# An expert's last tokens computed beside a full slot instead of in a slot of their own

## The chip, the cores and the metric

The kernel runs on one core of a Trainium2 chip. The metric is device time in microseconds. Engines: PE (TensorE, matrix products; PEld is its weight load), ACT (ScalarE), DVE (VectorE), POOL (GpSimd, which here issues indirect DMAs: gathers and scatters by a list of rows), SP (SyncE, which issues the plain DMAs). A name with q (SPq, PEldq) is an engine's queue of instructions: branches, register loads, semaphores.

## What is computed

The reference chains three stages: an attention with a feature map, a dense two-layer network, and a routed one (mixture of experts). The change touches the third alone:

```python
logits = x @ w_gate + modality_bias[modality_id]     # 4608 tokens, 8 experts
e_idx = np.argmax(logits, axis=1)
...
for e in range(E):
    mask = e_idx == e
    h = np.maximum(x[mask] @ w1[e], 0.0)             # 512 -> 1024
    out[mask] = gate_w[mask, None] * (h @ w2[e])     # 1024 -> 512
```

All is float32. With the inputs of the reference the eight experts get 227, 0, 0, 1555, 0, 1831, 994 and 1 tokens.

## The kernel before

Attention and the dense network run first, to about 1300 us. While the last unit of the dense network ends, the tokens are sorted into a table in DRAM, `tab`, one region of rows for each expert, a row being a token's number and its weight. Empty rows carry the number of a token that doesn't exist; its gather reads zeros and its scatter is dropped.

The routed stage works through 25 slots (`NS1`), of up to 256 tokens of one expert each (`T`). A slot is either full, 256 tokens wide, or half, 128 wide. `order` (from L587, on DVE) works out from the eight counts, by some 40 small operations, which expert and which region of `tab` each slot has, and leaves them in `ie` and `io`; `ni` holds how many full and half slots there are. An expert's tokens go into as many full slots as they fill; a rest of at most 128 tokens becomes a half slot, a longer one a full slot. Full slots come first, and 18 slots run whatever the counts (`NS0`). Each later slot stands in a `tc.If` whose condition every engine reads from `ni`: slots 18 to 20 exist in both forms, the full one first (L854) and the half one (L856); slots 21 to 24 in the half form alone. With these inputs there are 18 full slots and three half ones, 18, 19 and 20.

To float32 accuracy each operand is split into a high and a low part (`h`, `l`), and a product is three matmuls. For a slot that means:
- `gather(i)`: SP loads the slot's table rows `mrec`, POOL gathers 256 tokens (two indirect DMAs of 256 KB, `xg`);
- `prep(i)`: eight transposes on PE (`px`), cast and subtraction on ACT and DVE (`xT`);
- `fetch`: 4 MB of weights of the slot's expert by eight plain DMAs from SP into `raw`; `split_steps`: ACT casts each piece to `m` (L658) and DVE subtracts (L659), and after each second one SP issues the fetch of a later slot;
- `body(i)`: 96 matmuls of the first layer (`mh`, L699) and 48 of the second (`po`, L711), 128 of the slot's tokens after the other; ACT scales the output (`o`, L748), POOL scatters it (L749);
- `half(i)`: 24 matmuls of the first layer (`sh`, L724), with ACT's `sr`, eight transposes (`st`), 24 of the second (`sp`, L743).

`hooks(i)` interleaves with slot i's steps the gather for slot i+2, the splits for slot i+1 and, three steps before the end, `prep(i+1)`. The order on each engine is not written out by hand: a scheduler places the instructions of each straight stretch by their data and a model of their times, so that a longer chain on one engine can move others. `tc.If` bounds such a stretch. At an If that is not taken, an engine waits until what it has in flight is done (SP: until its DMAs have landed) and then branches over the block.

Of the kernel before, what the change touches and what calls it, by code (L numbers as in the profile page):

```python
# [940 lines left out]
```

## Time and profile before

| | us |
|---|---|
| median of 3 runs | 1830.23 (1829.14 to 1831.64) |
| profiled execution | 1822.83 |
| its span in the trace | 1820.8 |
| PE busy in the span | 1754.4 (96%) |

The profiled execution is one run with the hardware profiler; all times of rows count from its span's start. Its own time is 7.4 us under the median of the runs. 192.25 MB are moved. Of the 25 slots 21 run: L699 has 1728 matmuls, 96 for each of 18 full slots, and L724 has 72, 24 for each of three half slots. The routed stage's slots 2 to 17 lie between about 1380 and 1756 us, the half slots from 1757 us to the end.

### The profile page before, as it was taken

Reading aid. Unit: us, or ns where it says so; the run is one execution under the profiler, and the core shown is the slowest. Engines: PE = TensorE matmul, PEld = TensorE weight load, DVE = VectorE, ACT = ScalarE, POOL = GpSimd, SP = SyncE. Lnnn points to the kernel's source line nnn. Section 1 sums busy time; section 2 is a strip of 40 time slices with the busy share of each in tenths; the row PEclk is TensorE's granted clock in tenths of the full one; section 3 lists DMA queues with packets and bytes.
Section 4 is the critical chain, followed back from the end, with each engine's and each line's share of the span. In section 5 each row is a group of like instructions: output and inputs, shape, how many; then the busy total and the mean of one; then the engine's idle time right before and its main releaser. Section 6 shows DMA issues by size and latency. Waiting matters only on the chain. (4 is left out here: it accounts for less than half of the span.)

```text
span 1820.8 us, 27482 instructions
## 1 busy us (share of the span) xinstructions
PE 1754.4 (96%) x10038; PEld 1504.2 (83%) x10038; DVE 1110.5 (61%) x1959; ACT 942.9 (52%) x1715; POOL 644.6 (35%) x524
## 2 busy tenths in 40 slices
PE   8999999998789999999999999999898999999996
PEld 7999999997668888888888888888687999999974
DVE  6888877779895454545454545454546655655555
ACT  5777777776643433333433333433426555655555
POOL 0544454447554242425243424242322221211121
PEclk9999999999999999999999999999899999999998
DMA  6334333322420101010101000010309765766666
GB/s 177 108 99 125 109 85 104 102 85 87 132 77 1 47 1 47 1 47 1 46 1 37 11 23 25 18 30 18 122 36 366 274 222 197 248 224 225 230 217 221
DMA packets 143444, 192.25 MB, mean 106 GB/s; under 512 B 64831, under 2 KB 89535, under 8 KB 143298
## 3 DMA queue, kind: packets, MB, share of 16 engines
q1 hardware_dynamic: 135346, 168.82, 28.6%
q0 software_dynamic: 7952, 21.54, 3.6%
q8 instruction: 85, 1.39, 0.3%
q14 instruction: 61, 0.50, 0.1%
HBM read 160.61 MB, written 30.50 MB: 105 GB/s over the span
## 5 line engine op out<-in xcount | busy, mean ns | idle before, releaser
L450 PE MATMUL ph<-x,w 128*128 128x512 f32 x1728 | 429.6, 396 | 11.9 <-DVE fr L468 10.6
L450 PEld LDWEIGHTS ph<-x,w 128*128 128x128 f32 x1728 | 322.8, 189 | 90.0 <-DVE fr L468 13.9
L480 PE MATMUL acc<-gh,w 128*128 128x512 f32 x1152 | 357.2, 392 | 1.6 <-DVE gh L470 1.6
L471 POOL TENSOR_TENSOR gl<-fr,gh 128x512 fp32r<-128x512 f32 x144 | 187.8, 1305 | 360.0 <-DVE gh L470 291.9
L659 DVE TENSOR_TENSOR m<-raw,m 128x512 fp32r<-128x512 f32 x336 | 218.5, 690 | 137.4 <-ACT m L658 133.6
L480 PEld LDWEIGHTS acc<-gh,w 128*128 128x128 f32 x1152 | 218.0, 189 | 47.0 <-DVE gh L470 1.8
L480 PE MATMUL acc<-gl,w 128*128 128x512 f32 x576 | 226.9, 395 | 11.5 <-POOL gl L471 11.5
L658 ACT CAST m<-raw 128x512 fp32r<-128x512 f32 x336 | 195.5, 618 | 74.0 <-PE mh L699 30.3
L463 ACT ACTIVATE n<-ph 128x512 int32<-128x512 f32 x144 | 85.7, 595 | 257.4 <-PE ph L450 254.1
L699 PEld LDWEIGHTS mh<-xT,m 128*128 128x128 f32 x1728 | 210.0, 192 | 3.0 <-DVE m L659 1.2
L699 PE MATMUL mh<-xT,m 128*128 128x256 f32 x1728 | 210.9, 283 | 0.8 <-DVE m L659 0.4
L465 DVE SCALAR_TENSOR_TENSOR fr<-ph,n 128x512 f32<-128x512 f32 x144 | 99.2, 689 | 179.6 <-ACT n L463 177.2
L468 DVE SCALAR_TENSOR_TENSOR fr<-fr,ph 128x512 f32<-128x512 f32 x144 | 98.8, 686 | 164.7 <-ACT fr L467 164.5
L711 PE MATMUL po<-m,hh 128*128 128x512 f32 x576 | 180.9, 395 | 0.0
L466 ACT ACTIVATE fr<-fr 128x512 f32<-128x512 f32 x144 | 91.0, 632 | 147.2 <-DVE fr L465 143.3
L168 PEld LDWEIGHTS kv<-v,ke 128*128 128x128 f32 (+1 forms) x1280 | 146.0, 191 | 13.0 <-issue 7.1
L168 PE MATMUL kv<-v,ke 128*128 128x65 f32 (+1 forms) x1280 | 151.6, 273 | 1.7 <-ACT ke L148 1.6
L749 POOL DMA_INDIRECT out_dram<-o,mrec x39 | 39.6, 1015 | 295.5 <-ACT o L748 247.3
L223 PE MATMUL pn<-qx,kvz 128*128 128x288 f32 x512 | 136.6, 409 | 3.3 <-DVE kvz L179 1.8
L480 PEld LDWEIGHTS acc<-gl,w 128*128 128x128 f32 x576 | 109.5, 190 | 36.0 <-POOL gl L471 13.2
L711 PEld LDWEIGHTS po<-m,hh 128*128 128x128 f32 x576 | 105.9, 189 | 20.1
L223 PEld LDWEIGHTS pn<-qx,kvz 128*128 128x128 f32 x512 | 93.5, 192 | 24.9 <-ACT w L420 2.2
(200 smaller groups left out, 2782.4 us busy)
## 6 DMA issues: line engine op xcount, KB each, us to landing
raw<-in_moe_w_dram SPq DMA_DIRECT2D x179, 512.0 KB
xt<-xo SPq DMA_DIRECT2D x16, 576.0 KB
xr<-xt SPq DMA_DIRECT2D x36, 256.0 KB
raw_k<-in_k_dram SPq DMA_DIRECT2D x32, 256.0 KB
raw_q<-in_q_dram SPq DMA_DIRECT2D x32, 256.0 KB
v<-in_v_dram SPq DMA_DIRECT2D x64, 128.0 KB
st<-in_moe_w_in_dram SPq DMA_DIRECT2D x16, 512.0 KB
st<-in_moe_w_out_dram SPq DMA_DIRECT2D x16, 512.0 KB
```

The costliest lines, as they stand in the source:

```text
L168: nc.tensor.matmul(o,e[p0:p1,idx*256+s*F:idx*256+(s+1)*F],vh[p0:p1,h,cc,:],start=first and h==0 and s==0,stop=last,skip_group_check=True)
L223: nc.tensor.matmul(pn,kz[:,s,h*P:(h+1)*P],qx[:,h,s,su],start=s==0,stop=s==1)
L450: nc.tensor.matmul(ph,A[:,ws],xhl[u,d][k],start=n[0]==0,stop=n[0]==11); n[0]+=1
L465: nc.vector.scalar_tensor_tensor(g,ph,INV2PI,n,op0=ALU.mult,op1=ALU.subtract)
L466: nc.scalar.activation(g,g,AF.Sin,scale=math.pi)
L468: nc.vector.scalar_tensor_tensor(g,g,-0.5,ph,op0=ALU.add,op1=ALU.mult)
L471: nc.gpsimd.tensor_tensor(gl,g,f32(gh),ALU.subtract)
L480: nc.tensor.matmul(accs[u][d],A[:,ws],B,start=(f==0 and k==0),stop=(f==NF-1 and k==2))
L658: nc.scalar.copy(h,a)
L659: nc.vector.tensor_tensor(l,a,f32(h),ALU.subtract)
L699: nc.tensor.matmul(ph[:,f2*T:(f2+1)*T],A[:,ws],B[d//2][:,xs],start=n==0,stop=n==11); n+=1
L711: nc.tensor.matmul(po[c],A[:,ws],B,start=(f==0 and j==0),stop=(f==NF2-1 and j==2))
```

## The change

A rest of at most 128 tokens no longer has a slot of its own where its expert's last full slot is one of the slots 14 (`NX`) to 21: it is computed by a half, `half(i,True)`, that stands in an If right ahead of that slot's `body(i)` (from slot 18 on within the full form's If) and uses the same split weights. `order` sorts the slots into three classes, plain full, full with a rest beside, and half, by tables of 24 entries instead of 16 (some 75 operations, the wide ones cut in two). With these inputs slots 16 and 17 get the rests of 39 and 19 tokens, slot 18 stays a half slot with its one token, and slots 19 and 20 are empty. For slots 14 to 17 `gather` gets a third indirect DMA of 256 KB (`xgx`), and `prep_x` adds four transposes (`pxx`), a cast and a subtraction, whether the half runs or not. The full forms of slots 18 to 21 hold a half too; slot 21 has a full form now.

```diff
-    NS0=NTOK//T; NS1=NS0+NE-1; NSH=(NTOK+NE*(T//2-1))//T-NS0
+    NS0=NTOK//T; NS1=NS0+NE-1; NSH=(NTOK+NE*(T//2-1))//T+1-NS0; NX=14
+    NI=2+NS0-NX+NSH
...
+        at=[0]; room=xtile("fr","order",F32); ge=xtile("fr","order_ge",F32)[0:1,0:13*24].rearrange("p (s k) -> p s k",k=24)
+        def part(w):
+            at[0]+=w
+            return room[0:1,at[0]-w:at[0]]
+        e=part(25); nc.vector.memset(e[:,24:25],0.0)
+        for j in range(3): nc.vector.tensor_copy(e[:,8*j:8*j+8],ei)
         nc.vector.tensor_scalar(ki,ki,0xffff,None,op0=ALU.bitwise_and)
...
+        d=part(8); nc.vector.tensor_tensor(d,tot,nb,ALU.subtract)
+        lo=part(8); nc.vector.memset(lo,1.0); nc.vector.memset(lo[:,0:1],3.0)
+        hx=part(8); nc.vector.tensor_tensor(hx,nb,lo,ALU.is_ge)
+        nc.vector.tensor_tensor(hx,hx,d,ALU.mult)
+        ha=part(8); nc.vector.scalar_tensor_tensor(ha,nb,1.0,d,op0=ALU.is_lt,op1=ALU.mult)
+        nc.vector.tensor_tensor(nb,tot,ha,ALU.subtract); nc.vector.tensor_tensor(nb,nb,hx,ALU.subtract)
...
+        cv=part(1); nc.vector.tensor_reduce(cv,tt,AX.X,ALU.max)
+        kx=part(8); nc.vector.tensor_tensor(kx,px,cv.to_broadcast([1,8]),ALU.is_ge)
+        n=part(24)
+        nc.vector.tensor_tensor(n[:,8:16],kx,hx,ALU.mult)
+        nc.vector.tensor_copy(n[:,16:24],ha)
+        nc.vector.tensor_tensor(nb,nb,hx,ALU.add)
+        nc.vector.scalar_tensor_tensor(n[:,0:8],n[:,8:16],-2.0,nb,op0=ALU.mult,op1=ALU.add)
...
-        for i in (1,2,4,8):
-            t2=small(f"on{i}",0,[1,16]); nc.vector.tensor_copy(t2[:,0:i],end[:,0:i])
-            nc.vector.tensor_tensor(t2[:,i:16],end[:,i:16],end[:,0:16-i],ALU.add)
+        for i in (1,2,4,8,16):
+            t2=part(24); nc.vector.tensor_copy(t2[:,0:i],end[:,0:i])
+            nc.vector.tensor_tensor(t2[:,i:24],end[:,i:24],end[:,0:24-i],ALU.add)
             end=t2
...
         for d_,s_ in ((de,se),(do,so)):
-            nc.vector.tensor_tensor(ge,C["slot"].unsqueeze(2).to_broadcast([1,NS1,16]),end.unsqueeze(1).to_broadcast([1,NS1,16]),ALU.is_ge)
-            nc.vector.tensor_tensor(ge,ge,d_.unsqueeze(1).to_broadcast([1,NS1,16]),ALU.mult)
-            nc.vector.tensor_reduce(s_,ge,AX.X,ALU.add)
+            for s0,s1 in ((0,13),(13,NS1)):
+                g=ge[:,0:s1-s0,:]
+                nc.vector.tensor_tensor(g,C["slot"][:,s0:s1].unsqueeze(2).to_broadcast([1,s1-s0,24]),end.unsqueeze(1).to_broadcast([1,s1-s0,24]),ALU.is_ge)
+                nc.vector.tensor_tensor(g,g,d_.unsqueeze(1).to_broadcast([1,s1-s0,24]),ALU.mult)
+                nc.vector.tensor_reduce(s_[:,s0:s1],g,AX.X,ALU.add)
...
+        ni=small("ni",0,[1,NI],I32)
+        nc.vector.tensor_copy(ni[:,0:1],end[:,15:16]); nc.vector.tensor_copy(ni[:,1:2],end[:,23:24])
+        for n0,n1,i0,k0,k1 in ((2,2+NS0-NX,NX,7,15),(2+NS0-NX,NI,NS0,15,23)):
+            h=part(n1-n0); nc.vector.tensor_scalar(h,C["slot"][:,i0:i0+n1-n0],end[:,k0:k0+1],None,op0=ALU.is_ge)
+            h2=part(n1-n0); nc.vector.tensor_scalar(h2,C["slot"][:,i0:i0+n1-n0],end[:,k1:k1+1],None,op0=ALU.is_lt)
+            nc.vector.tensor_tensor(ni[:,n0:n1],h,h2,ALU.mult)
...
+    def rest(i): return NX<=i<NS0+NSH
+    def alloc_x(i):
+        X["x",i]=tuple(xtile("n",f"xX{k}_{i}") for k in range(2))
     def alloc_g(i):
-        R[i]=sb.tile([P,2,2],I32,tag="mrec",name=f"mrec_{i}",bufs=4)
+        R[i]=sb.tile([P,3,2],I32,tag="mrec",name=f"mrec_{i}",bufs=4)
+        if rest(i): xgs["x",i]=xtile("fr",f"xgx_{i}",F32)
         if i==1:
             xg=S("raw_k","xg_1",F32); xgs[i]=[xg[:,c*512:(c+1)*512] for c in range(2)]
         else: xgs[i]=[xtile("x1T",f"xg_{i}_{c}",F32) for c in range(2)]
-    def gather(i):
+    def gather(i,beside):
         rec=R[i]
-        nc.sync.dma_start(rec,tab[ds(off_[i],T),:].rearrange("(c p) t -> p c t",p=P))
+        nch=3 if beside else 2
+        nc.sync.dma_start(rec[:,0:nch,:],tab[ds(off_[i],nch*P),:].rearrange("(c p) t -> p c t",p=P))
+        if beside: nc.gpsimd.indirect_dma_start(xgs["x",i],None,x1d[:,:],IndirectOffsetOnAxis(ap=rec[:,2,0:1],axis=0))
         for c in range(2):
             nc.gpsimd.indirect_dma_start(xgs[i][c],None,x1d[:,:],IndirectOffsetOnAxis(ap=rec[:,c,0:1],axis=0))
     def prep(i):
...
                     nc.tensor.transpose(pt[:,d*T+c*P:d*T+(c+1)*P],xg[c][:,(2*g+d)*P:(2*g+d+1)*P],ident)
             nc.scalar.copy(h[g],pt)
             nc.vector.tensor_tensor(l[g],pt,f32(h[g]),ALU.subtract)
+    def prep_x(i):
+        h,l=X["x",i]; xg=xgs["x",i]
+        pt=ms(f"pxx_{i}")
+        for d in range(4): nc.tensor.transpose(pt[:,d*P:(d+1)*P],xg[:,d*P:(d+1)*P],ident)
+        nc.scalar.copy(h,pt)
+        nc.vector.tensor_tensor(l,pt,f32(h),ALU.subtract)
...
-    def half(i):
-        xh,xl=X[i]
+    def half(i,beside):
+        if beside:
+            h,l=X["x",i]; x=lambda d: (h[:,d*P:(d+1)*P],l[:,d*P:(d+1)*P])
+        else:
+            h,l=X[i]; x=lambda d: tuple(t[d//2][:,(d%2)*T:(d%2)*T+P] for t in (h,l))
         rs=[]
         for fh in range(2):
             ph=bank("pj",f"sh_{i}_{fh}")
             n=0
             for d in range(4):
-                wh,wl=W[i,0][2*d+fh]; xs=slice((d%2)*T,(d%2)*T+P)
+                wh,wl=W[i,0][2*d+fh]; xh,xl=x(d)
                 for (A,B) in ((xh,wh),(xl,wh),(xh,wl)):
-                    nc.tensor.matmul(ph,A[d//2][:,xs],B,start=n==0,stop=n==11); n+=1
+                    nc.tensor.matmul(ph,A,B,start=n==0,stop=n==11); n+=1
             r=xtile("row",f"sr_{i}_{fh}",F32)
             nc.scalar.activation(r,ph,AF.Relu)
             rs.append(r)
...
             ws=slice((f%4)*P,(f%4+1)*P)
             for j,(A,B) in enumerate(((hh,wh),(hh,wl),(hl,wh))):
                 nc.tensor.matmul(po,A[:,ws],B,start=(f==0 and j==0),stop=(f==NF2-1 and j==2))
-            if f==NF2-1: finish(i,0,po)
+            if f==NF2-1: finish(i,2 if beside else 0,po)
             if f%2==1: yield
...
-    def tokens(i):
+    def tokens(i,beside):
         if i<NS0+2: alloc_g(i)
-        load_off(i); gather(i)
+        load_off(i); gather(i,beside)
...
-            if i+2<NS1: tokens(i+2)
+            if i+2<NS1: tokens(i+2,steps==12 and rest(i+2))
             if i<NS0: alloc(i+1)
+            if NX<=i+1<NS0: alloc_x(i+1)
...
         h[steps-3].append(lambda:prep(i+1))
+        if NX<=i+1<NS0: h[steps-3].append(lambda:prep_x(i+1))
...
     for i in range(1,NS0):
-        if i==NS0-1:
-            loaded=[value(o["n"][0:1,j:j+1],mybir.ALL_ENGINES,NS1,"only compared with constants") for j in range(2+NSH)]
+        if i==NX-1:
+            loaded=[value(o["n"][0:1,j:j+1],mybir.ALL_ENGINES,NS1,"only compared with constants") for j in range(NI)]
+        if i>=NX:
+            with tc.If(loaded[2+i-NX]>0): run(half(i,True),{})
         run(body(i,i),hooks(i,12))
     for i in range(NS0,NS1):
         if i+1<NS1: alloc(i+1)
         if i+2<NS1: alloc_g(i+2)
-        if i<NS0+NSH:
-            with tc.If(loaded[0]>i): run(body(i,i),hooks(i,12))
-        is_half=loaded[2+i-NS0]>0 if i<NS0+NSH else loaded[1]>i
-        with tc.If(is_half): run(half(i),hooks(i,8))
+        if rest(i):
+            with tc.If(loaded[0]>i):
+                alloc_x(i); prep_x(i)
+                run(half(i,True),{})
+                run(body(i,i),hooks(i,12))
+        is_half=loaded[2+NS0-NX+i-NS0]>0 if rest(i) else loaded[1]>i
+        with tc.If(is_half): run(half(i,False),hooks(i,8))
 @with_exitstack
```

On POOL, around the end of slot 1; `xg_2` and `xg_3` are the gathers for slots 2 and 3, `out` from `o_1` the scatters of slot 1's two outputs. Before:

```order
L676 DMA xg_2_0_12559<-x1d_66,mrec_2_12558 128x512
L676 DMA xg_2_1_12560<-x1d_66,mrec_2_12558 128x512
L676 DMA xg_3_0_12607<-x1d_66,mrec_3_12606 128x512
L676 DMA xg_3_1_12608<-x1d_66,mrec_3_12606 128x512
L749 DMA out_0_dram<-o_1_0_12755,mrec_1_11937 4608x512
L749 DMA out_0_dram<-o_1_1_12818,mrec_1_11937 4608x512
L676 DMA xg_4_0_12858<-x1d_66,mrec_4_12857 128x512
L676 DMA xg_4_1_12859<-x1d_66,mrec_4_12857 128x512
```

After:

```order
L716 DMA xg_2_0_12582<-x1d_66,mrec_2_12581 128x512
L716 DMA xg_2_1_12583<-x1d_66,mrec_2_12581 128x512
L798 DMA out_0_dram<-o_1_0_12778,mrec_1_11937 4608x512
L798 DMA out_0_dram<-o_1_1_12841,mrec_1_11937 4608x512
L716 DMA xg_3_0_12630<-x1d_66,mrec_3_12629 128x512
L716 DMA xg_3_1_12631<-x1d_66,mrec_3_12629 128x512
L716 DMA xg_4_0_12881<-x1d_66,mrec_4_12880 128x512
L716 DMA xg_4_1_12882<-x1d_66,mrec_4_12880 128x512
```

The two gathers for slot 3 have moved behind both of slot 1's scatters.

On PE, slot 3's transposes `px_3` (`mh_2` and `po_2` are slot 2's first and second layer). Before, in the middle of slot 2's last 24 matmuls:

```order
L711 MATMUL po_2_1_12982<-m2_3_11969,hh_2_1_12904 128x512 x2
L711 MATMUL po_2_1_12982<-m2_3_11969,hl_2_1_12905 128x512
L684 MATMUL px_3_0_13044<-ident_60,xg_3_0_12607 128x128
L684 MATMUL px_3_0_13044<-ident_60,xg_3_1_12608 128x128
L684 MATMUL px_3_0_13044<-ident_60,xg_3_0_12607 128x128
L684 MATMUL px_3_0_13044<-ident_60,xg_3_1_12608 128x128
L684 MATMUL px_3_1_13051<-ident_60,xg_3_0_12607 128x128
L684 MATMUL px_3_1_13051<-ident_60,xg_3_1_12608 128x128
L684 MATMUL px_3_1_13051<-ident_60,xg_3_0_12607 128x128
L684 MATMUL px_3_1_13051<-ident_60,xg_3_1_12608 128x128
L711 MATMUL po_2_1_12982<-m2_4_11970,hh_2_2_12938 128x512 x2
```

After, from the start of slot 2:

```order
L745 MATMUL mh_2_0_12851<-xT_2_0_12638,m0_0_11950 128x256 x3
L745 MATMUL mh_2_1_12902<-xT_2_0_12638,m0_0_11950 128x256 x3
L745 MATMUL mh_2_0_12851<-xT_2_0_12638,m0_2_11952 128x256 x2
L745 MATMUL mh_2_1_12902<-xT_2_0_12638,m0_2_11952 128x256
L745 MATMUL mh_2_0_12851<-xT_2_0_12638,m0_2_11952 128x256
L745 MATMUL mh_2_1_12902<-xT_2_0_12638,m0_2_11952 128x256 x2
L724 MATMUL px_3_0_13067<-ident_60,xg_3_0_12630 128x128
L745 MATMUL mh_2_0_12851<-xT_2_1_12639,m0_4_11954 128x256 x2
L745 MATMUL mh_2_1_12902<-xT_2_1_12639,m0_4_11954 128x256 x2
L724 MATMUL px_3_0_13067<-ident_60,xg_3_1_12631 128x128
L745 MATMUL mh_2_0_12851<-xT_2_1_12639,m0_4_11954 128x256
L745 MATMUL mh_2_1_12902<-xT_2_1_12639,m0_4_11954 128x256
```

They have moved from the second layer of slot 2 to behind 12 matmuls of its first.

On PE, from slot 13 to slot 14 (`po_13` is slot 13's second layer, `mh_14` slot 14's first). Before:

```order
L711 MATMUL po_13_1_15702<-m1_6_11964,hl_13_3_15693 128x512
L711 MATMUL po_13_1_15702<-m1_7_11965,hh_13_3_15692 128x512 x2
L711 MATMUL po_13_1_15702<-m1_7_11965,hl_13_3_15693 128x512
L699 MATMUL mh_14_0_15795<-xT_14_0_15586,m0_0_11950 128x256 x3
L699 MATMUL mh_14_0_15795<-xT_14_0_15586,m0_2_11952 128x256 x3
```

After, with the transposes of the 128 tokens beside and the If:

```order
L730 MATMUL pxx_14_15877<-ident_60,xgx_14_15354 128x128 x4
L757 MATMUL po_13_1_15801<-m1_5_11963,hl_13_2_15758 128x512
L757 MATMUL po_13_1_15801<-m1_6_11964,hh_13_3_15791 128x512 x2
L757 MATMUL po_13_1_15801<-m1_6_11964,hl_13_3_15792 128x512
L757 MATMUL po_13_1_15801<-m1_7_11965,hh_13_3_15791 128x512 x2
L757 MATMUL po_13_1_15801<-m1_7_11965,hl_13_3_15792 128x512
L575 TENSOR_LOAD ni_0_12572
L901 COMPARE_AND_BRANCH
L773 MATMUL sh_14_0_15902<-m0_0_11950,xX0_14_15685 128x512
L773 MATMUL sh_14_0_15902<-m0_0_11950,xX1_14_15686 128x512
L773 MATMUL sh_14_0_15902<-m0_0_11950,xX0_14_15685 128x512
```

Between the two slots there are now a register load, a branch and the half's matmuls `sh_14`; the eight transposes `px_14` stand a few rows ahead of `pxx_14`, as they did before.

## Rows read from the trace of the kernel before

**Rows 1.** Table by stretch: its length, busy PE, PEld, DVE, ACT, POOL; clock, DMA.

```profile
1639.60:1662.70 23.10, 23.10 (x152) 21.18 (x152) 13.78 (x23) 13.52 (x24) 4.20 (x5) 1.00 0.66 229
1757.40:1772.60 15.20, 13.53 (x64) 10.52 (x64) 12.23 (x20) 12.12 (x23) 4.54 (x3) 1.00 0.72 230
1772.60:1795.20 22.60, 15.79 (x64) 12.33 (x64) 12.31 (x20) 12.20 (x23) 3.93 (x3) 0.85 0.78 274
```

**Rows 2.** Waits, 1400 to 1757 us: who for whom, total us, times, longest.

```profile
PE mh L699 <- issue: 0.4, 1, 0.4
```

**Rows 3.** PE in order of time, slots 18 to 20: start, us, operation [idle before].

```profile
1757.44 5.71 PE L724 MATMUL sh<-m,xT 128*128 128x512 f32 x24 [1.28 <-ACTq L854]
1762.99 0.60 PE L732 MATMUL st<-ident,sr 128*128 128x128 f32 x4
1764.41 0.66 PE L732 MATMUL st<-ident,sr 128*128 128x128 f32 x4 [0.82 <-ACT sr L726]
...
1768.02 1.03 PE L684 MATMUL px<-ident,xg 128*128 128x128 f32 x8
1768.81 0.71 PE L743 MATMUL sp<-m,sg 128*128 128x512 f32 x2
...
1771.40 0.39 PE L743 MATMUL sp<-m,sl 128*128 128x512 f32 x1
1772.66 0.73 PE L724 MATMUL sh<-m,xT 128*128 128x512 f32 x2 [0.87 <-ACTq L854]
...
1813.60 0.39 PE L743 MATMUL sp<-m,sl 128*128 128x512 f32 x1
```

**Rows 4.** ACT in order of time, slot 19's weight splits.

```profile
1778.57 3.74 ACT L658 CAST m<-raw 128x512 fp32r<-128x512 f32 x7 [6.01 <-SPq L854]
```

**Rows 5.** PE in order of time, end of slot 1 to slot 3.

```profile
1367.03 0.62 PE L711 MATMUL po<-m,hh 128*128 128x512 f32 x2
...
1375.06 0.48 PE L684 MATMUL px<-ident,xg 128*128 128x128 f32 x1 [7.19 <-DMA xg<-x1d,mrec]
1376.40 1.75 PE L684 MATMUL px<-ident,xg 128*128 128x128 f32 x7 [0.87 <-DMA xg<-x1d,mrec]
1377.81 1.20 PE L711 MATMUL po<-m,hh 128*128 128x512 f32 x2
...
1381.65 1.23 PE L699 MATMUL mh<-xT,m 128*128 128x256 f32 x9
...
1405.63 0.64 PE L699 MATMUL mh<-xT,m 128*128 128x256 f32 x4
```

**Rows 6.** ACT in order of time, slot 1's second output.

```profile
1382.28 0.70 ACT L748 ACTIVATE o<-po,mrec 128x512 f32<-128x512 f32 x1
```

**Rows 7.** POOL in order of time, the gathers for slots 2 and 3.

```profile
1368.25 0.97 POOL L676 DMA_INDIRECT xg<-x1d,mrec  x1 [5.95 <-DMA mrec<-tab]
1369.53 0.96 POOL L676 DMA_INDIRECT xg<-x1d,mrec  x1 [0.30 <-issue]
1377.52 1.23 POOL L676 DMA_INDIRECT xg<-x1d,mrec  x1 [7.03 <-PE px L684]
```

**Rows 8.** DVE and POOL in order of time, end of `order`, last table scatter.

```profile
1355.20 0.22 DVE L624 TENSOR_SCALAR io<-so,ob 1x25 int32<-1x25 f32 x1
...
1361.34 0.96 POOL L562 DMA_INDIRECT tab<-rec,pi  x1 [3.61 <-DMA tab<-rec,pi]
```

**Rows 9.** The Ifs' lines: engine, operation, count, ns least/median/most, first and last start.

```profile
L854 SPq EVENT_SEMAPHORE  x27: 17/17/17, 1747.9 to 1798.0; - x27
...
L854 PEldq COMPARE_BRANCH  x3: 338/377/3351, 1753.2 to 1791.1; - x3
...
L856 SPq COMPARE_BRANCH  x10: 38/42/45, 1754.1 to 1818.5; - x10
...
L856 PEldq COMPARE_BRANCH  x10: 70/193/3307, 1757.2 to 1815.2; - x10
...
L856 PEldq EVENT_SEMAPHORE  x4: 51/51/51, 1814.0 to 1818.6; - x4
```

More of the change, by code (lines that the diff above doesn't have):

```diff
@@ L598, in order @@
+        for j in range(3): nc.vector.tensor_copy(e[:,8*j:8*j+8],ei)
         nc.vector.tensor_scalar(ki,ki,0xffff,None,op0=ALU.bitwise_and)
-        n=small("on0",0,[1,16])
+        q=[]
         for j,more in ((0,T//2-1),(1,T-1)):
-            kj=small(f"ki{j}",0,[1,8],I32); nc.vector.tensor_scalar(kj,ki,8*more,None,op0=ALU.add)
+            kj=part(8).bitcast(I32); nc.vector.tensor_scalar(kj,ki,8*more,None,op0=ALU.add)
             nc.vector.tensor_scalar(kj,kj,11,None,op0=ALU.logical_shift_right)
-            nc.vector.tensor_copy(n[:,8*j:8*j+8],kj)
@@ L604, in order @@
-        nc.vector.tensor_tensor(n[:,8:16],n[:,8:16],n[:,0:8],ALU.subtract)
-        b=small("ob",0,[1,17]); nc.vector.tensor_scalar(b,e,float(REG),None,op0=ALU.mult)
+            q.append(part(8)); nc.vector.tensor_copy(q[j],kj)
+        nb,tot=q
+        d=part(8); nc.vector.tensor_tensor(d,tot,nb,ALU.subtract)
+        lo=part(8); nc.vector.memset(lo,1.0); nc.vector.memset(lo[:,0:1],3.0)
+        hx=part(8); nc.vector.tensor_tensor(hx,nb,lo,ALU.is_ge)
+        nc.vector.tensor_tensor(hx,hx,d,ALU.mult)
@@ new lines, in order @@
+        ha=part(8); nc.vector.scalar_tensor_tensor(ha,nb,1.0,d,op0=ALU.is_lt,op1=ALU.mult)
+        nc.vector.tensor_tensor(nb,tot,ha,ALU.subtract); nc.vector.tensor_tensor(nb,nb,hx,ALU.subtract)
+        px=hx
+        for i in (1,2,4):
+            t2=part(8); nc.vector.tensor_copy(t2[:,0:i],px[:,0:i])
+            nc.vector.tensor_tensor(t2[:,i:8],px[:,i:8],px[:,0:8-i],ALU.add)
+            px=t2
+        pl=part(8); nc.vector.tensor_tensor(pl,nb,hx,ALU.subtract)
+        tt=part(2); nc.vector.tensor_reduce(tt[:,0:1],pl,AX.X,ALU.add)
@@ L624, in order, with load_off @@
         nc.vector.tensor_scalar(io,so,b[:,0:1],None,op0=ALU.add)
-        ni=small("ni",0,[1,2+NSH],I32)
-        nc.vector.tensor_copy(ni[:,0:1],end[:,7:8]); nc.vector.tensor_copy(ni[:,1:2],end[:,15:16])
-        h=small("oh0",0,[1,NSH]); nc.vector.tensor_scalar(h,C["slot"][:,NS0:NS0+NSH],end[:,7:8],None,op0=ALU.is_ge)
-        h2=small("oh1",0,[1,NSH]); nc.vector.tensor_scalar(h2,C["slot"][:,NS0:NS0+NSH],end[:,15:16],None,op0=ALU.is_lt)
-        nc.vector.tensor_tensor(ni[:,2:2+NSH],h,h2,ALU.mult)
+        ni=small("ni",0,[1,NI],I32)
[4 more added lines that the diff above has]
+            nc.vector.tensor_tensor(ni[:,n0:n1],h,h2,ALU.mult)
         o.update(e=ie,off=io,n=ni)
     def load_e(i): e_[i]=value(o["e"][0:1,i:i+1],SP,NE-1,"an expert")
-    def load_off(i): off_[i]=value(o["off"][0:1,i:i+1],SP,NE*REG-T,"inside the table by construction")
+    def load_off(i): off_[i]=value(o["off"][0:1,i:i+1],SP,NE*REG-T-P,"inside the table by construction")
     W={}
@@ L802, in moes @@
             for i in range(2):
-                alloc_g(i); gather(i)
+                alloc_g(i); gather(i,False)
             alloc_w()
@@ L820, in moes @@
              4:[lambda:rows(u,0)],5:[lambda:pe(u),lambda:rows(u,1)],6:[lambda:rows(u,2)],7:[lambda:rows(u,3),lambda:route1(u)],
-             9:[lambda:route2(u)],10:[lambda:prep(1)],11:[order,lambda:tokens(2),lambda:load_e(2),lambda:load_e(3),lambda:weights(8,12)]})
+             9:[lambda:route2(u)],10:[lambda:prep(1)],11:[order,lambda:tokens(2,False),lambda:load_e(2),lambda:load_e(3),lambda:weights(8,12)]})
     def hooks(i,steps):
```

13 lines of the change are left out of this document (7 added, 6 removed).

## Prediction

> **What bounds the kernel now.** I read the table of stretches first. In a full slot of the routed stage, TensorE (PE) is busy all 23.10 of 23.10 us at full clock while the DMA engines are busy 0.66 of the time; in the stretch of slot 18 it is busy 13.53 of 15.20 us, in that of slot 19 only 15.79 of 22.60 us at a granted clock of 0.85 [rows 1]. So full slots cost PE time and the last half slots cost something else. The list of waits between 1400 and 1757 us says how strict the first part is: PE's only wait there is 0.4 us in all [rows 2]. Whatever delays PE before 1400 us is therefore carried to the end undiminished.
>
> Next the order of time on PE in slot 18, a half slot that runs undisturbed: 24 matmuls from 1757.44, four transposes at 1762.99, a wait of 0.82 us, four more, 24 matmuls, among them the next slot's eight px transposes (1768.02 to 1768.81, 0.79 us), the last start at 1771.40. Slot 19 starts at 1772.66 [rows 3]. What stretches slots 19 and 20 is told by ACT: its weight splits stand still 6.01 us until SP lets them go at 1778.57 [rows 4]. SP stands at a full-slot If that is not taken, and there it waits until the weight loads in flight have landed. The last matmul starts at 1813.60 [rows 3] and the span ends at 1820.8: 7 us of branches and closing semaphores. From slot 18's start to the end are 63.4 us.
>
> **Routing.** Counts of tokens per expert from the reference's inputs are 227, 0, 0, 1555, 0, 1831, 994, 1. Before: 18 full slots and three half slots (rests of 39 and 19 tokens, and the single token). After: the same 18 full slots, the rests of 39 and 19 beside slots 16 and 17, and one half slot, 18. Slots 19 and 20 go, with their two weight sets.
>
> **The change part by part.** The sum is made against the profiled execution, 1822.83 us, which lies 7.4 us under the median of the runs, 1830.23. I add that back at the end.
>
> *Slots 1 to 3, by the new order: +9.0.* The diff does nothing here but lengthen the DVE chain of `order`, yet the scheduler, which also places by that chain, moves two things. On POOL the two gathers for slot 3 now stand behind slot 1's second scatter, and on PE slot 3's transposes px stand inside slot 2's first layer, behind 12 of its 96 matmuls, where before they stood in its second layer. Step by step:
> - PE meets the wait for slot 2's gathers as before, at 1375.06 (7.19 us of idleness) and 1376.40 [rows 5]. Four matmuls that came after it now come ahead, under the wait, so slot 1 ends not at 1381.65 but some 1.2 us earlier, 1380.4.
> - ACT's output activation followed PE's end by 0.63 us (1382.28) and took 0.70 [rows 6]; so it ends at 1381.7. The scatter takes about 1.0 like the other POOL issues [rows 7], to 1382.7, and 0.30 later (the gap at 1369.53) slot 3's first gather is issued at 1383.0, where before it was issued at 1377.52. The second follows after the 1.23 us seen there and a gap of 0.30: 1384.5.
> - Gathers issued at 1368.25 and 1369.53 released PE at 1375.06 and 1376.40 [rows 5, 7], 6.8 and 6.9 us after the issue began. So slot 3's rows are there at 1389.8 and 1391.4.
> - PE does 12 matmuls of slot 2 and stands from about 1382.6. At 1391.4, 80 first-layer and 48 second-layer matmuls and seven transposes are left. The undisturbed slot took 23.98 us (1381.65 to 1405.63) [rows 5] with 0.79 of transposes in it; less the 16 matmuls already done (2 us) that leaves 21.6, to 1413.0. After a wait of this kind PE ran at half speed: a pair of matmuls that took 0.62 at 1367.03 took 1.20 at 1377.81 [rows 5]. Some 2 us are lost so, an estimate from the four pairs and singles behind that row and the transposes ahead of it. Slot 3 starts at 1414.6 to 1415 instead of 1405.63: +9.0 to 9.4; I take 9.0. Bounds: 7, if ACT is free sooner and the slow clock costs nothing; 11, if ACT's splits stand ahead of the output.
>
> Here the row and a page differ. The two gathers above took 6.8 us, with the DMA engines loading weights at the same time. The Trainium skill (DMA: Bandwidth & Descriptors, Anatomy of one DMA — SWDGE (gpsimd) path) gives about 2.0 us plus the bytes at 436 GB/s; for 256 KB that is an estimate of 2.6 us, and by it this term would be +4.8 and the sum +2.7. I go by the rows, which are the same transfer in the same stretch.
>
> *The `order` chain itself: nothing.* It grows from some 40 to 75 small DVE operations. Its result io, ready at 1355.4, is ready around 1362 to 1363.5; but slot 2's table rows can only be loaded after the last table scatter issued at 1361.34 has landed [rows 8], and the gather at 1368.25 waited for exactly that load [rows 7]. What DVE delays in slot 1 meanwhile lies under PE's 7.19 us. If that cover fails it costs 1 to 2 us.
>
> *Slots 14 to 17.* Each has four more transposes: eight take 0.79, so 4 x 0.4 = +1.6 (1.2 to 1.8). Their gather of 256 KB, cast and subtraction lie beside a busy PE: ACT and DVE are busy 13.5 and 13.8 of 23.1 us [rows 1]. Ifs stand ahead of all four bodies. Two are not taken; there PE waits for its own last matmul, loads a register and branches. The gaps between PE's stretches at such places are 0.87 us at 1772.66 and 1.28 at 1757.44 [rows 3]: 2 x 0.9 = +1.8 (0.8 to 2.6). SP has nothing to wait for in these Ifs. Two are taken: each half without px is 14.2 - 0.8 = 13.4 us, or 12.9 where the 0.82 us wait of slot 18 goes, since no weight splits stand in the new block ahead of ACT's sr: 2 x 13.2 = +26.4 (25.6 to 28).
>
> *From slot 18 to the end: 63.4 becomes 31.5, -31.9.* Slot 18 itself stays. Behind it stand nine Ifs that are not taken where four stood behind slot 20, and there are two paths through them. SP: it is released 21.1 us after slot 18's start (1778.57 less 1757.44, [rows 3, 4]) as now, then passes eight more Ifs at an estimated 0.75 us (nine semaphores each: 27 at three Ifs, [rows 9]; the bounds are 0.4 and 0.9), and closes in 2.3 (from its last branch at 1818.5 to the end): 29.4 us. PE: 14.2 us of slot 18, then jumps over three full blocks, each now about 450 instructions (transposes, half and body), and six halves. A jump usually costs PE 0.07 to 0.4 us, but once on each of the two lines 3.3 us [rows 9]: at 1753.2, hidden under matmuls queued before, and in the tail at 1815.2, in the open. With three or four of those, nine passes at 0.4 and a close of 2.2 (from PE's last semaphore at 1818.6), PE's path is 30 to 33.5 us. I take 31.5; bounds 29.4 and 34.
>
> The Trainium skill (Runtime: NRT & Kernel Launch, Instruction fetch mechanics) says that a taken branch whose target lies outside the window already fetched waits for a fetch. The two rows of 3.3 us agree; the two other jumps over a full body, at 0.34 and 0.38 us, show that not each one pays.
>
> **Sum.** 9.0 + 1.6 + 1.8 + 26.4 - 31.9 = +6.9 us: 1829.7 for a profiled execution like the one shown, 1837 as a median.
>
> **The rivals.**
> - *No stall in slot 2, not slower.* Decided at 1383 to 1391 us: if slot 3's gather lands by the time that PE reaches px, that is within 1 us of its issue, or is issued before slot 1's scatter after all, the 9.0 go and the sum is -2.1: 1828. For it speaks only that the 6.8 us were measured with the queues full; against it that they are full at the later place too, and POOL's order. The page's 2.6 us lies between: 1833.
> - *The cheap tail.* Instruction fetch keeps ahead, as it did in two of three jumps over a body, and SP's path decides: 2.1 us less, 1835.
> - *Jumps that cost at the new Ifs too.* Four Ifs in the middle of the PE-bound stretch, each with a jump or a return: three or four fetches of 3.3 us in the open add 10 us: 1847. Against it: a half is some 130 instructions, and jumps over halves took 0.07 to 0.4 in all but one case of ten.
> - *The change does what it says and no more.* Two half slots of 22.6 and 19.8 us [rows 1] replaced by 26.4 us beside, without stall or dearer tail: -14, 1816. It needs the first two rivals at once, and the three extra fetches not to exist.
>
> **How the numbers follow.** Forecast 0.58, no stall 0.17, cheap tail 0.12, dear jumps 0.11, the pure gain 0.02. A measurement of this kernel tells 0.2%, 3.7 us, from no change: faster is below 1826.6, slower above 1833.9. The forecast's own span by its bounds is 1832 to 1843, nearly all slower; cheap tail splits about 3 to 2; dear jumps are slower; no stall is mostly the same, a quarter faster. Together: slower 0.70, same 0.23, faster 0.07. The range reaches from the no-stall case to the forecast's upper bound, 1828 to 1843.
>
> **What would show it.** Right: PE waits 5 to 8 us for xg in slot 2 between 1382 and 1392, and slot 3 starts near 1414.6; slots 16 and 17 with their halves take 36 to 37 us without a wait of PE above 1 us; slot 18 starts about 39 us later than before, near 1796, and the span ends 30 to 33 us after it, with PE branches of 3.3 us behind the last matmul. About 8 MB less is moved. Wrong: slot 3 starting within 2 us of 1405.6; branches of 3 us in front of slots 14 to 18; PE idle in front of the beside halves because xgx or its split comes late.

## The result, and the profile of the changed kernel

The changed kernel is slower: median 1855.1 us of four runs (1852.0 to 1857.4) against 1829.7 us before, ratio 1.014, 95% interval 1.0125 to 1.0154. That is +25.4 us, where +6.9 was forecast; the time lies outside the range. The profiled execution took 1851.99 us with a span of 1850.1; it moved 184.51 MB, 7.7 MB less.

The experiments ran later, on three chips (most on chip 5, the rest on chips 6 and 15). On each of them the kernel before takes 1822 to 1823 us; the changed one, run once more on chip 5, takes 1850.2. So each run is compared with runs of the kernel before beside it on the same chip.

Where the time went, read from the starts of PE's slots in the two profiles, and in that of the changed kernel with the addresses of before (run `e3_addresses_as_before`, below). The first column of numbers is a time, the others are differences to it:

| stretch | before, us | forecast | changed | changed, addresses as before |
|---|---|---|---|---|
| start to slot 1 | 1348.0 | 0 | +8.9 | -0.7 |
| slot 1 to slot 3 | 57.6 | +9.0 | +9.5 | +8.6 |
| slot 3 to slot 13 | 233.8 | 0 | +2.0 | -0.1 |
| slot 13 to slot 18 | 118.0 | +29.8 | +32.9 | +31.8 |
| slot 18 to the end | 63.4 | -31.9 | -24.1 | -23.8 |
| sum | 1820.8 | +6.9 | +29.3 | +15.8 |

(The difference of the profiles, 29.3 us, is 4 us above that of the medians, since the profiled execution of before lies 6.9 us under the median of its four runs and the changed one's 3.1 us.)

**Slots 1 to 3.** PE in order of time in the changed kernel; compare [rows 5]:

```profile
1385.81 0.69 PE L724 MATMUL px<-ident,xg 128*128 128x128 f32 x2 [7.95 <-DMA xg<-x1d,mrec]
...
1393.05 0.51 PE L745 MATMUL mh<-xT,m 128*128 128x256 f32 x2 [2.32 <-ACT m L692]
1393.94 2.50 PE L745 MATMUL mh<-xT,m 128*128 128x256 f32 x10 [0.39 <-DVE m L693]
1399.83 0.45 PE L724 MATMUL px<-ident,xg 128*128 128x128 f32 x1 [3.38 <-DMA xg<-x1d,mrec]
...
1401.34 0.48 PE L724 MATMUL px<-ident,xg 128*128 128x128 f32 x1 [0.20 <-DMA xg<-x1d,mrec]
...
1424.01 2.19 PE L745 MATMUL mh<-xT,m 128*128 128x256 f32 x17
```

POOL in the changed kernel, the gathers for slots 2 and 3 around slot 1's scatters; compare [rows 7]:

```profile
1378.98 0.98 POOL L716 DMA_INDIRECT xg<-x1d,mrec  x1 [6.57 <-DMA mrec<-tab]
1380.26 0.96 POOL L716 DMA_INDIRECT xg<-x1d,mrec  x1 [0.30 <-issue]
1381.53 1.01 POOL L798 DMA_INDIRECT out_dram<-o,mrec  x1 [0.30 <-issue]
1391.74 1.00 POOL L798 DMA_INDIRECT out_dram<-o,mrec  x1 [9.20 <-ACT o L797]
1393.04 1.11 POOL L716 DMA_INDIRECT xg<-x1d,mrec  x1 [0.30 <-issue]
1394.45 1.49 POOL L716 DMA_INDIRECT xg<-x1d,mrec  x1 [0.30 <-issue]
```

The gathers for slot 3 stand behind the scatter that waited 9.20 us for slot 1's output, and PE waits for them inside slot 2's first layer. From issue to PE's release they take 6.8 us (1393.04 to 1399.83) and 6.9 (1394.45 to 1401.34), the durations of [rows 5, 7]. In this stretch the DMA engines are busy throughout (share 1.04) and PE, between its waits, runs at a granted clock of about 0.5, which is 1.2 GHz:

```profile
1393.00:1401.00 8.00, 4.18 (x17) 3.54 (x17) 5.10 (x9) 3.64 (x7) 2.60 (x2) 0.53 1.04 398
```

A second wait is new: 2.32 us at the start of slot 2, for a weight split on ACT. ACT's order has moved too. Before, ten of slot 2's weight pieces were cast ahead of `xT`, the last three at 1377.70; in the changed kernel four, and ACT then stands 4.17 us until PE's transposes come:

```profile
1382.78 1.14 ACT L692 CAST m<-raw 128x512 fp32r<-128x512 f32 x2 [0.23 <-DMA raw<-in_moe_w_dram]
1388.08 1.23 ACT L725 CAST xT<-px 128x512 fp32r<-128x512 f32 x2 [4.17 <-PE px L724]
```

**The middle.** PE from slot 14 to slot 18 (`pxx` and the half beside, `sh<-m,xX`):

```profile
1707.78 0.66 PE L730 MATMUL pxx<-ident,xgx 128*128 128x128 f32 x4
...
1711.38 11.77 PE L745 MATMUL mh<-xT,m 128*128 128x256 f32 x96 [1.33 <-ACTq L901]
...
1735.64 5.65 PE L773 MATMUL sh<-m,xX 128*128 128x512 f32 x24
...
1742.02 0.66 PE L781 MATMUL st<-ident,sr 128*128 128x128 f32 x4 [0.30 <-ACT sr L775]
...
1772.70 5.63 PE L773 MATMUL sh<-m,xX 128*128 128x512 f32 x24
...
1810.80 5.71 PE L773 MATMUL sh<-m,xT 128*128 128x512 f32 x24 [1.60 <-PEq L907]
```

The untaken If ahead of slot 15 leaves PE idle for 1.33 us at 1711.38; ahead of the halves at 1735.64 and 1772.70 there is no wait at all. The wait at the untaken If is not PE's own. Its register load and its branch come early, at 1707.82 and 1708.24, while matmuls are still queued, and its last matmul ends at 1710.06. (So the wait stands behind the branch, and not ahead of it as the section on the kernel before has it.) It then waits until ACT has passed the same If, at 1711.32, behind slot 14's output and one more weight split:

```profile
1710.09 0.69 ACT L797 ACTIVATE o<-po,mrec 128x512 f32<-128x512 f32 x1
1710.68 0.61 ACT L692 CAST m<-raw 128x512 fp32r<-128x512 f32 x1
```

PE's own branches at these Ifs are short, 0.23 and 0.35 us where they jump over a half:

```profile
L901 PEldq COMPARE_BRANCH  x6: 70/176/353, 1682.5 to 1781.3; - x6
```

**The end.** The branches of the two lines of trailing Ifs; compare [rows 9]:

```profile
L907 PEldq COMPARE_BRANCH  x4: 2937/4212/6386, 1806.1 to 1838.1; - x4
```

```profile
L912 SPq COMPARE_BRANCH  x8: 34/45/50, 1807.6 to 1837.8; - x8
...
L912 PEldq COMPARE_BRANCH  x8: 77/955/2651, 1810.6 to 1846.4; - x8
...
L912 PEldq EVENT_SEMAPHORE  x6: 51/51/51, 1831.7 to 1849.0; - x6
```

PE's jumps over the full forms take 2.9 to 6.4 us each (the first, at 1806.1, begins under matmuls queued before, and PE then stands 1.60 us, to 1810.80); those over halves up to 2.65. SP passes its last If at 1837.8, and ACT, DVE and POOL are not later; PE passes its last semaphore at 1849.0. The 11 us between are PE's alone.

**Everything ahead of slot 1.** The same matmuls of the dense stage, 600 to 1200 us, in groups by shape (count in the window, busy us, mean ns of one), before:

```profile
L480 PE MATMUL acc<-gh,w 128*128 128x512 f32 x823 | 253.6, 389 | 0.0
L480 PE MATMUL acc<-gl,w 128*128 128x512 f32 x411 | 160.0, 389 | 0.0
```

and in the changed kernel:

```profile
L480 PE MATMUL acc<-gh,w 128*128 128x512 f32 x810 | 252.2, 392 | 0.0
L480 PE MATMUL acc<-gl,w 128*128 128x512 f32 x405 | 159.1, 393 | 0.0
```

In the same 600 us it gets through 810 and 405 instead of 823 and 411, and each lasts 392 to 393 ns instead of 389. The stretch 600 to 900 has a granted clock of 1.00 (the 2.4 GHz level) and PE busy all the time, as before:

```profile
600.00:900.00 300.00, 299.82 (x1378) 241.72 (x1377) 142.12 (x252) 113.03 (x181) 106.63 (x84) 1.00 0.07 24
```

No instruction of this stage is touched by the change.

### The profile page after: what moved, and what is told of

Read it like the earlier page. It is cut to its first block, busy times and chain, and to the rows that moved or that the text cites. A ratio compares the mean times of both kernels' runs of the same rounds, so it can differ in the third digit from the quotient of the medians.

```text
span 1850.1 us, 27395 instructions
## 1 busy us (share of the span) xinstructions
PE 1769.3 (96%) x10038; PEld 1504.9 (81%) x10038; DVE 1098.0 (59%) x1964; ACT 926.8 (50%) x1683; POOL 646.6 (35%) x526
## 2 busy tenths in 40 slices
DMA packets 140509, 184.51 MB, mean 100 GB/s; under 512 B 64831, under 2 KB 89535, under 8 KB 140354
## 5 line engine op out<-in xcount | busy, mean ns | idle before, releaser
L450 PE MATMUL ph<-x,w 128*128 128x512 f32 x1728 | 432.5, 398 | 12.2 <-DVE fr L468 10.4
L480 PE MATMUL acc<-gh,w 128*128 128x512 f32 x1152 | 361.1, 395 | 0.5 <-DVE gh L470 0.5
L693 DVE TENSOR_TENSOR m<-raw,m 128x512 fp32r<-128x512 f32 x304 | 200.3, 695 | 121.6 <-ACT m L692 119.4
L692 ACT CAST m<-raw 128x512 fp32r<-128x512 f32 x304 | 177.4, 618 | 57.7 <-PE mh L745 31.1
L168 PEld LDWEIGHTS kv<-v,ke 128*128 128x128 f32 (+1 forms) x1280 | 146.0, 191 | 12.9 <-issue 7.1
L757 PE MATMUL po<-m,hl 128*128 128x512 f32 x288 | 114.2, 396 | 0.0
```

Source lines behind the costliest of these rows:

```text
L168: nc.tensor.matmul(o,e[p0:p1,idx*256+s*F:idx*256+(s+1)*F],vh[p0:p1,h,cc,:],start=first and h==0 and s==0,stop=last,skip_group_check=True)
L450: nc.tensor.matmul(ph,A[:,ws],xhl[u,d][k],start=n[0]==0,stop=n[0]==11); n[0]+=1
L480: nc.tensor.matmul(accs[u][d],A[:,ws],B,start=(f==0 and k==0),stop=(f==NF-1 and k==2))
L692: nc.scalar.copy(h,a)
L693: nc.vector.tensor_tensor(l,a,f32(h),ALU.subtract)
L757: nc.tensor.matmul(po[c],A[:,ws],B,start=(f==0 and j==0),stop=(f==NF2-1 and j==2))
```

## The experiments

In this order: the stall in slot 2, the end, the unforeseen slower matmuls, and the sum of the parts.

### The stall in slots 1 to 3

Edit of the changed kernel: slot 1's scatters (`put`) are queued behind slot 3's gathers on POOL, slot 3's first transpose behind what stands ahead of it in the program on PE.

```diff
+            g3=nc.gpsimd.indirect_dma_start(xgs[i][c],None,x1d[:,:],IndirectOffsetOnAxis(ap=rec[:,c,0:1],axis=0))
+        G[i]=g3.ins
...
+        if i==1:
+            with tc.issue_after(G[3]): put()
+        else: put()
...
+                    if i==3 and g+d+c==0: tc.keep_in_program_order(tr)
```

> The changed kernel with three issue orders pinned as they were before the change: slot 3's two gathers ahead of slot 1's scatters on POOL, and slot 3's transposes on PE in slot 2's second layer. Theory (the scheduler's new order costs the stall in slot 2): slot 3 starts 8 to 10 us earlier than in the changed kernel, no wait of PE for slot 3's gather, and the time falls by 8 to 10 us, to about 1846. Rival (the longer chain of order() itself delays slot 2's gather, and the new order is only where that shows): slot 3 starts at most 2 us earlier, about 1853.

Measured: 1844.3 us, 21.1 over the kernel before (ratio 1.0112, 1.0095 to 1.0129), where the unedited changed kernel is 27.8 over (below): 6.7 us less, where 8 to 10 were expected. From slot 1 to slot 3 PE took 61.3 us; 67.1 and 66.1 in the two profiles of the changed kernel, 57.6 before. PE in this run, end of slot 1 and start of slot 2:

```profile
1382.02 0.69 PE L725 MATMUL px<-ident,xg 128*128 128x128 f32 x2 [6.35 <-DMA xg<-x1d,mrec]
...
1389.89 0.50 PE L747 MATMUL mh<-xT,m 128*128 128x256 f32 x2 [2.32 <-ACT m L692]
1390.79 13.15 PE L747 MATMUL mh<-xT,m 128*128 128x256 f32 x94 [0.39 <-DVE m L693]
```

The wait for slot 3's gather is gone, so that part of the theory holds. But 2.32 us for a split on ACT stay: the scheduler had moved ACT's work too, and that was not pinned. So 5 to 6 us of the stall belong to the two moved places that were priced. Some 1.5 to 4 us stay (other profiles of kernels with the order of before have 57.3 to 59.8 us in this stretch), 2.3 of them in this wait, at a third place that was not priced.

The other way round, the kernel before with a longer chain in `order`:

```diff
+        for _ in range(30): nc.vector.tensor_scalar(so,so,0.0,None,op0=ALU.add)
```

> The kernel before with 30 more small operations on DVE at the end of order(), which add zero; the scheduler then puts slot 3's gathers behind slot 1's scatters and slot 3's transposes into slot 2's first layer, as in the changed kernel. Theory (the longer chain moves them, and that costs the stall): 8 to 10 us slower than before, about 1839, with a wait of PE for slot 3's gather in slot 2. Rival (the stall in the changed kernel comes from something else that the change does): within 2 us of before.

Measured: 1831.7 us, +8.4 (ratio 1.0048, 1.0031 to 1.0064). PE in it:

```profile
1375.26 0.69 PE L685 MATMUL px<-ident,xg 128*128 128x128 f32 x2 [6.15 <-DMA xg<-x1d,mrec]
...
1383.21 0.62 PE L700 MATMUL mh<-xT,m 128*128 128x256 f32 x3 [2.32 <-ACT m L659]
...
1390.07 0.45 PE L685 MATMUL px<-ident,xg 128*128 128x128 f32 x1 [4.96 <-DMA xg<-x1d,mrec]
```

From slot 1 to slot 3 it takes 66.8 us, 9.2 more than before. The same waits stand at the same places, though nothing but the length of a chain of small DVE operations has changed. Slot 2's gather is no later than before (PE is released at 1375.26, before at 1375.06), so it is the order and not the chain's own time.

### The end

Edit of the changed kernel: the loop over the slots behind 17 ends with slot 18.

```diff
-    for i in range(NS0,NS1):
+    for i in range(NS0,NS0+1):
```

> The changed kernel without the code of slots 19 to 24, which are empty with these inputs (it would leave out tokens with other inputs); slot 18 still loads the weights for the slots behind it. Theory (PE's jumps over the blocks that don't run, each waiting for instructions, set the end): from slot 18's first matmul to the end 22 to 24 us instead of 39.3, so 15 to 17 us less, about 1839. Rival (the weight loads in flight, which SP waits for, set the end, and PE's jumps only fill that time): at most 5 us less, about 1850.

Measured: 1830.0 us, +6.7 over before (ratio 1.0035, 1.0022 to 1.0048), 21 us less than the unedited kernel's 27.8, where 15 to 17 were expected. From slot 18's first matmul (1806.4) to the end 21.5 us instead of 39.3. (The profiled executions of this run and of the changed kernel on the same chip differ by 18.9 us; 17.9 of them lie here.) The loads in flight still land, and SP still waits for them, so in the changed kernel they were not what set the end: PE's jumps were. With the jumps gone the loads come next: the DMA engines are busy until about 1824 us, SP's closing waits begin to pass at 1826.05, and without the loads the stretch takes 17.6 us (the run with all mended, below).

What the jumps wait for can be read from the changed kernel's trace. Among its DMA packets are transfers of kind `instruction`, 16 KB each on queue q8; from 1820 to 1850 us there are nine:

```profile
q8 instruction: 9, 0.15, 2.1%
```

Each of the seven long jumps behind slot 18, 1.6 to 6.4 us, ends 1.35 to 1.51 us after such a transfer has landed. So does the jump at 1806.1, and so do the two of 3.3 us in the kernel before (1.36 and 1.33 us). The short jumps, 0.22 and 0.25 us here, show no such wait. So the long jumps wait for code; that q8 is PE's queue is concluded from these times alone. The longest jump is not long by its block: its transfer starts 3.9 us after the jump, while the DMA engines are full of weights (share 1.03 from 1824 to 1828 us). The one of 4.6 us has two transfers.

### The slower matmuls

The change moves `order`'s small tiles into the shared pool; the pools allocated behind them, with attention's tiles and the weights of both networks, lie 2528 bytes a partition lower. Edit of the changed kernel, which puts them back:

```diff
+        pad=small("pad",0,[1,632])
```

> The changed kernel with 2528 bytes a partition of unused space in the pool of small tiles, so that the pools behind it (attention, dense stage, weights of the routed stage) lie at the addresses they have in the kernel before; order and work are the same. Theory A (in the changed kernel a 128x512 matmul follows the last after 230 ns on average instead of 227 because its operands lie elsewhere): the pitch goes back to 227 ns, the dense stage ends 8 us earlier, about 1846. Theory B (the pitch varies from run to run, whatever the kernel): no change beyond 3 us, about 1855, and the pitch differs between profiles of kernels with equal addresses.

Measured: 1838.7 us, +15.5 over before (ratio 1.0084, 1.0067 to 1.0101). The dense stage in it:

```profile
L480 PE MATMUL acc<-gh,w 128*128 128x512 f32 x824 | 253.7, 389 | 0.0
L480 PE MATMUL acc<-gl,w 128*128 128x512 f32 x412 | 160.4, 389 | 0.0
```

389 ns, and the counts of before within one. The changed kernel itself, once more:

> The changed kernel once more, beside the kernel before on one chip and beside the next three. Theory A (its pitch of matmuls comes from its addresses): the same pitch as in its first profile (median 229 ns in the dense stage, 600 to 900 us, where the kernel before has 227), slot 1 starts 7 to 9 us later than in the kernel before, 1.3 to 1.5% slower. Theory B (by chance of the run): a pitch of 227 ns, about 0.9% slower.

Measured: 1850.2 us (ratio 1.0157, 1.0140 to 1.0174), +27.8; its pitch (the time from one matmul's start to the next) has a median of 229 ns over all of PE's matmuls from 600 to 900 us, as in its first profile, and 227 in the kernel before. So the addresses are worth 12 us of it, 27.8 less 15.5. Now the kernel before with only its addresses moved: `order`'s small tiles as pieces of two tiles of the shared pool, as in the changed kernel, same operations, same issue order.

```diff
-        e=small("oe",0,[1,17])
+        pad=small("pad",0,[1,8])
+        room=xtile("fr","order",F32)
+        e=part(17)
...
-        ge=small("ge",0,[1,NS1,16])
+        ge=xtile("fr","order_ge",F32)[0:1,0:NS1*16].rearrange("p (s k) -> p s k",k=16)
```

> The kernel before with the small tiles of order() put into two tiles of the shared pool, so that the pools behind the small tiles lie 2528 bytes a partition lower, as in the changed kernel; issue order and work are the kernel before's. Theory A (addresses): 8 to 11 us slower than before, a median pitch of 229 ns in the dense stage. Theory B: within 2 us of before, 227 ns.

Measured: 1832.2 us, +9.8 (ratio 1.0058, 1.0041 to 1.0075).

```profile
L480 PE MATMUL acc<-gh,w 128*128 128x512 f32 x816 | 254.1, 392 | 0.0
L480 PE MATMUL acc<-gl,w 128*128 128x512 f32 x409 | 160.6, 393 | 0.0
```

The same edit with no `pad`, 32 bytes further:

> The same as the run that moves the pools by 2528 bytes, without 32 bytes of it: the pools lie 2560 bytes lower, a multiple of 64, so that their start is again 32 bytes off a multiple of 64, as in the kernel before. Theory A1 (what counts is the address within 64 bytes): within 2 us of before, 227 ns. Theory A2 (what counts is the distance to something else, or a longer period): 4 us or more slower. Theory B: within 2 us of before in both.

Measured: 1822.9 us (ratio 1.0000, 0.9991 to 1.0010).

```profile
L480 PE MATMUL acc<-gh,w 128*128 128x512 f32 x824 | 253.8, 389 | 0.0
L480 PE MATMUL acc<-gl,w 128*128 128x512 f32 x412 | 160.4, 389 | 0.0
```

Two kernels that differ in nothing but 32 unused bytes a partition are 9.3 us apart. Theory B is out. Which places are fast? With a longer `pad`:

```diff
-        pad=small("pad",0,[1,8])
+        pad=small("pad",0,[1,16])
```

> The kernel before with its pools 2496 bytes lower: 64 bytes more than the run that moved them by 2560, so their start lies 32 bytes off a multiple of 64 but not of 128. Theory A1 (the place within 64 bytes decides): within 2 us of before, a median pitch of 227 ns. Theory A2 (the place within 128 bytes or more decides): 4 us or more slower, 229 ns.

Measured: 1832.0 us (ratio 1.0052, 1.0031 to 1.0072). A1 is wrong. With 32 and with 24 elements in place of the 16:

> The kernel before with its pools 2432 bytes lower: 128 bytes more than the run that moved them by 2560, so their start lies 32 bytes off a multiple of 128 but not of 256. Theory A3 (the place within 128 bytes decides): within 2 us of before, 227 ns in the dense stage. Theory A4 (a period of 256 bytes or more): 4 us or more slower, 229 ns.

> The kernel before with its pools 2464 bytes lower, their start on a multiple of 128. With the runs at 32, 64 and 96 bytes off one this is the fourth place that the allocator gives within 128 bytes. Theory (the kernel before lies at the one fast place, 32): 4 us or more slower, 229 ns or more. Rival (the start of a 128-byte piece is as fast, or faster): within 2 us of before, or faster.

Measured: 1830.9 us (1.0050, 1.0033 to 1.0067) and 1832.6 us (1.0053, 1.0036 to 1.0070). In all three slow runs a matmul of the dense stage lasts 392 to 393 ns. A3 is wrong too: the run moved by 2432 lies at the same place within 128 bytes as the kernel before and is slow. Of six places tried two are fast, 2560 bytes apart. So if there is a period, it is longer than 128 bytes. What it is, and which operand's address counts, was not tried and stays open.

### The sum

The changed kernel with the pinned orders, the addresses of before, beside forms from slot 16 on (`NX=16`), no code behind slot 18 and no preparation for it in slot 18:

```diff
-NX=14
+NX=16
...
+        pad=small("pad",0,[1,640])
...
-    for i in range(NS0,NS1):
+    for i in range(NS0,NS0+1):
...
-        with tc.If(is_half): run(half(i,False),hooks(i,8))
+        with tc.If(is_half): run(half(i,False),{})
```

> The changed kernel with the issue orders pinned as before, the pools at the addresses of the kernel before, beside forms only in slots 16 and 17 (two Ifs and eight transposes less), and without the code of slots 19 to 24 and slot 18's preparation for them (with other inputs it would leave out tokens). By the parts measured so far: 5.8 (order) + 4.9 (two slots' Ifs and transposes) + 17.8 (tail) + about 1 below the 1838.7 of the kernel with only the addresses mended: about 1809, 14 us faster than before. If the tail is then bound by something else (the last output's way to DRAM), about 1815.

Measured: 1806.0 us, 16.4 faster than before (ratio 0.9909, 0.9892 to 0.9925). The parts add up to within about 3 us. Slot 18 to the end is 17.6 us here. But it lacks the code for other inputs, so its partner is the kernel before without the code behind slot 20:

```diff
-    for i in range(NS0,NS1):
+    for i in range(NS0,NS0+3):
...
-        with tc.If(is_half): run(half(i),hooks(i,8))
+        with tc.If(is_half): run(half(i),hooks(i,8) if i<NS0+2 else {})
```

> The kernel before without the code of slots 21 to 24 and without slot 20's preparation for them (with other inputs it would leave out tokens): the fair partner of the run with all mended. Theory: slot 20's loads no longer have to land and PE no longer jumps: 3 to 5 us less, about 1818.5; the mended change is then still about 12 us faster than its partner. Rival: the half slots 18 and 19, which wait for loads in flight, hold most of it and the end costs nothing: within 1 us of before.

Measured: 1814.7 us, 8.0 faster than before by the medians and 10.4 by the ratio (0.9943, 0.9924 to 0.9963), twice what was expected or more: without loads and splits for a slot that doesn't come, slot 20 itself takes 12.9 us to its last matmul instead of 18.8. So computing the rests beside full slots is worth some 6 to 8 us by itself (16.4 less 8.0 by the medians, 6 by the ratios); the two intervals together leave 1.5 to 11, so that it is a gain at all is shown, its size is not. And the mended kernel with all its code, that is without the last two of the edits shown above:

> The kernel of the run with all mended, but with all its code behind slot 18, so that it is complete for any routing: issue orders and addresses as before, beside forms from slot 16 on. Theory: the tail of nine untaken Ifs comes back whole, from slot 18's first matmul to the end 39 to 40 us, so about 22 us slower than the run with all mended: about 1828, 5 us slower than before. Rival (the tail is shorter where less went before it): 1820 or less.

Measured: 1829.4 us, +6.7 (ratio 1.0034, 1.0023 to 1.0045), as expected: from slot 18's first matmul to the end 39.3 us, and the tail takes back 23 us and the whole gain with it. A complete version that beats the kernel before was not found; the tail of untaken Ifs would have to go first.

## Why the prediction was wrong

Two terms failed: one that the sum did not have, for what the change doesn't touch, and the count and price of the jumps at the end. Either of them alone (6.9 + 10.9 or 6.9 + 7.8) puts the time beyond the range, whose upper end lies 12.8 us over 1830.2.

- **The sum had no term for what the change doesn't touch.** The largest miss, 10.9 us of the 22.4 by which the difference of the two profiles exceeds the forecast (18.5 by the medians), lies ahead of slot 1 (8.9) and in the untouched slots 3 to 13 (2.0). The diff takes tiles out of a pool, and that was read as no work ("does nothing here but lengthen the DVE chain"). The moved pool shows in the edit (`small(...)` becomes `part(...)`); its price shows in no row of before. No rival held it.
- **The end: the step "three or four of those".** SP's path was sized right: its last branch is at 1837.8, 2.3 us of closing make 1840.1, 29.3 us after slot 18's first matmul, forecast 29.4. PE's path was said to be 30 to 33.5 us and is 39.3. Nine jumps took 23.7 us, 1821.96 to 1849.05 with the passes between, of which 3.2 lie under the last matmuls. Seven of the nine were long, not three or four, and the long ones took 1.6 to 6.4 us, not 3.3: 6.4, 2.9 and 4.6 over full forms, 2.65, 2.4, 1.6 and 2.6 over halves. One ground for the low count was a row misread. Of the ten branches of [rows 9] on L856 only four jump over a half, with 0.23, 0.43, 0.21 and 3.31 us; the others enter a half that runs or leave it. So one case in four had been dear, not "one case of ten". The Trainium skill (Runtime: NRT & Kernel Launch, Instruction fetch mechanics) has a taken branch wait for a fetch where its target lies outside the fetched window; the trace agrees for the seven long jumps, which end 1.35 to 1.51 us after a 16 KB instruction transfer, and the two of 0.22 and 0.25 us did not wait. It was the rule that spoke against this change; the forecast gave too much weight to the two short jumps over a body before.
- **Slots 1 to 3: +9.5 against +9.0, right in the wait but not in its size; that the sum fits is partly luck.** The gathers took the forecast 6.8 and 6.9 us; the Trainium skill's formula (DMA: Bandwidth & Descriptors, Anatomy of one DMA — SWDGE (gpsimd) path) gives an estimate of 2.6 for them and holds at neither place, with the DMA engines loading weights alongside. But PE waited 3.6 us for them, not 7: it came there later, after 2.32 us for ACT's split, since ACT's order had moved as well, and ran at a granted clock of about 0.5 from 1393 to 1403 us. Only POOL and PE were priced.
- **The `order` chain: right.** With the addresses of before, io was ready at 1361.3 and the load of slot 2's table rows was issued at 1364.2, 2.9 us later.
- **Slots 13 to 18: +31.8 (addresses of before) against +29.8.** Right in the main, with no wait ahead of the halves, as forecast. The untaken Ifs were sized 0.9 us and cost 1.4 to 1.5: slots 13 and 14 take 25.6 us, slot 15, with the same transposes but a taken If behind it, 24.1. PE's idle gap of 1.33 to 1.38 is nearly all of it, and it is ACT that PE waits for, not its own register load and branch. The transposes, sized 0.4 a slot, come with 0.7 to 0.8 (24.0 to 24.1 us instead of 23.3); why they cost more than their own 0.4 is open. The halves were 12.7 us, a little less than the 13.2. The rival of dear jumps at the new Ifs did not come: 0.23 and 0.35 us.
- **The direction** was right, and so was giving the rival "not slower" little.

## What to carry to other kernels

A change that takes or adds a small tile moves every pool behind it: compare the durations of a matmul that the change does not touch, before and after, ahead of anything else, and pad the pool so that addresses stay while you measure. Compare the issue order on every engine and price every piece that moved, not only the two that look dear. Code that doesn't run has a price where engines jump over it one block after another: count the untaken blocks behind the last useful instruction, and look in the trace for instruction transfers beside long branches. When a row counts branches, sort them into those that jump over a block and those that enter or leave one.
